# Three moves in the tail of a two-batch layer: tap loads behind the next copy, the next batch's gradient rows loaded mid-tail, the norm's shift a half step ahead

## The chip, the cores and the metric

One core of a Trainium2 chip runs the whole program. The metric is device time in microseconds (us). A run here means one kernel on one chip: one profiled execution and, where I timed it, several more. "Ratio" is the mean time of a kernel's fast executions over the mean of those of the kernel before in the same rounds, so not quite the ratio of the medians that I quote.

## The reference

The reference is the forward pass of one layer and its gradients by `jax.vjp` (x and grad_out of 2 x 4000 x 144, bf16, five taps):

```python
xa = _layernorm(x)                       # (B, T, D) = (2, 4000, 144)
q, k, v = split(xa @ w_qkv)
glob = softmax(q @ k.T * D**-0.5) @ v @ w_att_out
u, g = split(gelu(xa @ w_mlp_in))
loc = (u * depthwise5(_layernorm(g), dw_csgu)) @ w_mlp_out
m = concatenate([glob, loc])
m = m + depthwise5(m, dw_merge)
out = x + m @ w_merge
# returned: out, and the gradients of out against grad_out for x and seven weights
```

## The kernel before

Each batch passes three phases: a head (norm, transposes, taps of the gradient rows), attention (by far the longest, TensorE nearly without a hole: busy 449 of the 460 us from 100 to 560), and a tail, which forms out, the gradient of x and sums for the weights. The tail walks over 16 pairs of 128 rows in half steps `h`; two half steps are a group `g`. These are the parts the change and the argument touch (cuts marked with ...):

```python
def fill(g):                                   # "tap loads"
    for h in range(2):
        r_ = G["r", h, g] = wk.tile([128, 512], BF, tag="r80_%d" % h, name="r80")
        taps[h].load(r_[0:80, :], g * 512, 512, nc.scalar)

def put(g):                                    # the stores they read back
    for h in range(2):
        taps[h].store(G["rs", h][112:128, :], g * 512, 512, nc.scalar)
...
for h in range(NPR + 5):
    g, hf = divmod(h, 2)
    if 0 < h < NPR:
        turn_dx2(*turn_dx(h))                  # 8 transposes, ScalarE copies them to hT
    if hf == 0 and g < NGR:
        turn(g, 0); corr(g, 0); turn(g, 1); corr(g, 1)     # (joined here)
    ...
    if 0 <= h - 1 < NPR:
        sums_act(h - 1); sums_dve(h - 1)
    if hf == 0 and g < NGR:
        put(g)
    if hf == 1 and 0 <= g - 1 < NGR:
        fill(g - 1)
    if nrm:                                    # the norm of the second batch
        for lag, f_ in ((4, nrm.apply), (3, nrm.power), (2, nrm.stats), (1, nrm.load)):
            q, m = divmod(h - lag, 2)
            if m == 0 and 0 <= q < NGR:
                f_(q)
        if NPR <= h < NPR + 3:
            take_go(k, nxt, 1, h - NPR, nrm.ld)  # gradient rows of the second batch
    ...
    if 0 <= h - 1 < NPR:
        means(h - 1)                           # GpSimd: cc, t
    if 0 <= h - 2 < NPR:
        fin(h - 2)                             # VectorE: dxo, then its store on SyncE
    ...
    if hf == 1 and g + 2 < NGR:
        load_dh(g + 2)                         # dhr rows, SyncE
        loads(g + 2)                           # gs and ug rows, SyncE
```

The head's first step for a group transposes the gradient rows `gs` (tile `pm`), has GpSimd extract the last 16 columns of the taps (`g`), transposes these and copies them (`go80f`).

## Time and profile before

| | |
|---|---|
| median, lowest, highest | 1293.03, 1292.06, 1295.48 us (3 executions) |
| profiled span | 1288.0 us |
| first tail, second head, second tail | 85.3, 31.8, 71.5 us |

I cut each trace at four TensorE instructions: the first EF product that waits for GpSimd's g (start of a tail), the head's first pm transpose, attention's first pD product, and the first fH product of the last phase that reads f_ETr. In the lines shown PE is TensorE, DVE VectorE, ACT ScalarE and POOL GpSimd; SPq and ACTq are transfers issued by SyncE and ScalarE; the bracket holds the idle time just before and what ended it.

### The profile page before, as it was taken

To read this page: it belongs to the slowest core of one execution; us is meant where nothing else is said; L and a number is where in the kernel's file an instruction comes from. 1 tells how busy PE (TensorE), PEld (TensorE's weight loads), DVE (VectorE), ACT (ScalarE), POOL (GpSimd) and SP (SyncE) were. 2 spreads that over 40 slices of the span, in tenths; PEclk is the share of its full clock that TensorE was granted. 3 is DMA by queue.
4 is the path that set the end of the run, shared out by engine and by line. 5 is a ranking of instruction groups with operands and counts; after the bars stand their busy time and mean duration, and the time that the engine had idled before them with its cause. 6 is when DMAs were issued, how large, how long until landed. Compare 5 with 4: busy or idle time off the path is not lost.

```text
span 1288.0 us, 39900 instructions
## 1 busy us (share of the span) xinstructions
PE 1211.8 (94%) x15116; PEld 949.9 (74%) x15116; DVE 962.3 (75%) x3293; ACT 843.5 (65%) x2498; POOL 558.8 (43%) x1033
## 2 busy tenths in 40 slices
PE   4899999999999999998989999999999999998996
PEld 2657777777777777788975777777777777778994
DVE  4656778888888788857735677888878878885674
ACT  2667777767767766546646767777777767664542
POOL 6412444545444453257611244444544445324650
PEclk9999999999999999999999999999999999999998
DMA  6378989898989989887775889899888999987861
GB/s 185 88 142 147 156 155 159 155 167 151 161 151 159 170 155 165 151 190 216 202 220 109 152 156 152 153 169 170 148 160 153 154 170 155 164 154 182 238 168 29
DMA packets 634223, 205.51 MB, mean 160 GB/s; under 512 B 577183, under 2 KB 631556, under 8 KB 633988
## 3 DMA queue, kind: packets, MB, share of 16 engines
q1 hardware_dynamic: 627472, 197.54, 80.6%
q10 hardware_dynamic: 6548, 5.33, 1.7%
q8 instruction: 120, 1.97, 0.6%
q14 instruction: 83, 0.68, 0.2%
HBM read 46.22 MB, written 21.79 MB: 53 GB/s over the span
## 4 chain that ended last, share of the span: by engine, by line
PE 71%; DVE 13%; DMA 4%; issue 4%; ACT 4%; POOL 3%; SPq 1%; ACTq 0%; DVEq 0%; POOLq 0%
PE y L1911 15%; PE pS L1865 9%; PE X L1933 9%; PE X L1934 8%; PE pD L1865 7%; PE pS L1861 5%; DVE Sm L1875 5%; PE pc L1573 3%; PE pb L1467 2%; PE po L2088 2%; PE EF L2063 1%; DVE jg L1792 1%; PE gr L2159 1%; DVE acc L1949 1%; ACT Qs L1894 1%
## 5 line engine op out<-in xcount | busy, mean ns | idle before, releaser
L1875 DVE SCALAR_TENSOR_TENSOR Sm<-pD,Pm 128x500 bf16<-128x500 f32 x512 | 325.7, 673 | 80.3 <-PE pD L1865 47.6
L1873 ACT ACTIVATE Pm<-pS 128x500 bf16<-128x500 f32 x512 | 295.5, 586 | 41.2 <-PE pS L1865 38.3
L1933 PE MATMUL X<-Qs,Sm 128*128 128x144 bf16 x2048 | 285.6, 226 | 9.3 <-DVE acc L1949 8.9
L1946 POOL TENSOR_TENSOR acc<-xs,acc 128x432 f32<-128x432 f32 x150 | 168.5, 1123 | 280.5 <-ACT xs L1945 280.0
L1934 PE MATMUL X<-Bt,Pm 128*128 128x144 bf16 x2048 | 285.4, 226 | 0.7 <-DVE Bt L1898 0.7
L1934 PEld LDWEIGHTS <-Pm 128*128 128x128 bf16 x2048 | 199.9, 98 | 11.9 <-issue 11.3
L1933 PEld LDWEIGHTS <-Sm 128*128 128x128 bf16 x2048 | 199.8, 98 | 1.5 <-issue 0.9
L1911 PEld LDWEIGHTS <-PT 128*128 128x128 bf16 x2048 | 136.5, 97 | 30.7 <-issue 2.4
L1911 PEld LDWEIGHTS <-ST 128*128 128x128 bf16 x2048 | 136.4, 97 | 27.6
L1945 ACT COPY xs<-X 128x432 f32<-128x432 f32 x150 | 77.9, 519 | 111.4 <-PE X L1934 103.4
L1949 DVE TENSOR_TENSOR acc<-X,acc 128x432 f32<-128x432 f32 x180 | 104.0, 578 | 53.9 <-PE X L1934 53.2
L1873 ACT ACTIVATION_READ_ACCUMULATOR Pm<-pS 128x1 f32 x512 | 105.0, 205 | 0.0
L1861 PE MATMUL pD<-rb,QBr 16*128 16x500 bf16 x448 | 96.0, 378 | 3.3 <-DVE Sm L1875 2.8
L1865 PEld LDWEIGHTS <-BTm 128*128 128x128 bf16 x512 | 49.8, 98 | 59.9 <-issue 1.6
L1861 PE MATMUL pS<-rb,QBr 16*128 16x500 bf16 x448 | 91.9, 380 | 0.1
L1792 DVE SCALAR_TENSOR_TENSOR jg<-gnC,dgC 128x256 bf16<-128x256 bf16 x160 | 89.6, 560 | 1.0
L1921 POOL TENSOR_TENSOR B_t<-zd,yd 128x144 bf16<-128x144 f32 x64 | 34.0, 531 | 113.0 <-ACT zd L1920 112.7
L1865 PEld LDWEIGHTS <-QTm 128*128 128x128 bf16 x512 | 29.1, 97 | 72.5 <-issue 72.5
L1865 PE MATMUL pS<-rb,QTm 128*128 128x500 bf16 x256 | 76.9, 382 | 0.0
L1865 PE MATMUL pS<-ra,QTm 128*128 128x500 bf16 x256 | 76.5, 381 | 0.0
L1911 PE MATMUL y<-rb,PT 128*128 128x144 bf16 x1024 | 74.3, 226 | 1.0 <-ACT zd L1920 1.0
L1911 PE MATMUL y<-ra,PT 128*128 128x144 bf16 x1024 | 74.3, 226 | 1.1 <-ACT zd L1920 1.1
(626 smaller groups left out, 2895.0 us busy)
## 6 DMA issues: line engine op xcount, KB each, us to landing
gs<-in_grad_out_dram SPq DMA_DIRECT2D x24, 720.0 KB
dh_d<-dh SPq DMA_DIRECT2D x32, 144.0 KB
dhr<-dh_d SPq DMA_DIRECT2D x16, 288.0 KB
gs<-in_grad_out_dram SPq DMA_DIRECT2D x8, 540.0 KB
xg<-in_x_dram SPq DMA_DIRECT2D x21, 144.0 KB
dug_d<-dug SPq DMA_DIRECT2D x16, 144.0 KB
dug<-dug_d SPq DMA_DIRECT2D x32, 72.0 KB
ug_d<-ug SPq DMA_DIRECT2D x32, 72.0 KB
```

Of the source, the lines that this page charges most:

```text
L1573: nc.tensor.matmul(pc[:, q, 0:128], t[:, q * 128 + m:q * 128 + m + 128], W.dg[:, (4 - m) if back else m, :], start=(m == 0), stop=(m == 4))
L1792: nc.vector.scalar_tensor_tensor(jg[:], a_[:, m:m + 256], 1.0, d_[:, 2:258], op0=ALU.mult, op1=ALU.mult, accum_out=dws[:, p, m:m + 1])
L1861: nc.tensor.matmul(o_[h][:, 0:SC], jt[i // 4][2][rr, i % 4, :], S.XR[c2][rr, 0:SC], start=True, stop=False)
L1865: nc.tensor.matmul(o_[h][:, 0:SC], jt[i // 4][w][:, i % 4, :], S.xaT[:, c0:c0 + SC], start=False, stop=True)
L1873: nc.scalar.activation(P[:, pb, c1:c1 + SC], o_[h][:, 0:SC], ACT.Exp, accum_out=ld8[:, 0, n_:n_ + 1])
L1875: nc.vector.scalar_tensor_tensor(Sm[:, pb, c1:c1 + SC], o_[h][:, 0:SC], 1.0, P[:, pb, c1:c1 + SC], op0=ALU.mult, op1=ALU.mult, accum_out=l ...
L1911: nc.tensor.matmul(y[:, w, :], src[:, jj, :], S.xaa[:, j, :], start=(j == 0), stop=(j == NBK - 1))
L1933: nc.tensor.matmul(X[:, jj, :], Sm[:, i % NP, j * 128:(j + 1) * 128], Qs[:, i % 4, :], start=(kk == 0 and jj == 0), stop=False, skip_group ...
L1934: nc.tensor.matmul(X[:, jj, :], P[:, i % NP, j * 128:(j + 1) * 128], Bt[:, i % 4, :], start=False, stop=(kk == 1), skip_group_check=True)
L1945: nc.scalar.copy(xs[:, 0:nj, :], X[:, 0:nj, :])
L1946: nc.gpsimd.tensor_tensor(a_, xs[:, 0:nj, :], a_, op=ALU.add)
L1949: nc.vector.tensor_tensor(a_, X[:, 0:nj, :], a_, op=ALU.add)
```

## The change

Its intent was to take three waits off TensorE's path: the copy of hT no longer stands behind a load on ScalarE, the second batch's rows are there when the head begins, and ScalarE's apply finds its shift ready.

```diff
+    def shift(self, g):
+        nc = self.k.nc
+        mv = self.t[g][1]
+        rs = self.S.rstd_x[:, g * 4:g * 4 + 4]
+        nm = self.sm.tile([128, 4], F32, tag="nmx", name="nm")
+        self.t[g].append(nm)
+        nc.vector.scalar_tensor_tensor(nm[:], mv[:, :, 0], -1.0, rs, op0=ALU.mult, op1=ALU.mult)
+
     def apply(self, g):
         nc = self.k.nc
-        xg, mv = self.t.pop(g)
+        xg, mv, nm = self.t.pop(g)
         rs = self.S.rstd_x[:, g * 4:g * 4 + 4]
-        nm = self.sm.tile([128, 4], F32, tag="nmx", name="nm")
-        nc.vector.scalar_tensor_tensor(nm[:], mv[:, :, 0], -1.0, rs, op0=ALU.mult, op1=ALU.mult)
...
                 nrm.power(g)
+                nrm.shift(g)
                 nrm.apply(g)
...
                     turn_dx2(*turn_dx(h))
+                if hf == 0 and 0 <= g - 2 < NGR:
+                    fill(g - 2)
...
-                if hf == 1 and 0 <= g - 1 < NGR:
-                    fill(g - 1)
...
-                    for lag, f_ in ((4, nrm.apply), (3, nrm.power), (2, nrm.stats), (1, nrm.load)):
+                    for lag, f_ in ((5, nrm.apply), (4, nrm.shift), (3, nrm.power), (2, nrm.stats), (1, nrm.load)):
...
-                    if NPR <= h < NPR + 3:
-                        take_go(k, nxt, 1, h - NPR, nrm.ld)
+                    if h in (9, 11, 13):
+                        take_go(k, nxt, 1, (h - 9) // 2, nrm.ld)
```

Lines of the tail stand 7 further down in the changed kernel: L2063 of before is L2070 of after.

## The prediction

> **What bounds the kernel now.** I began with the page's busy table, which says that TensorE is the bound for the kernel as a whole.
>
> ```profile
> span 1288.0 us, 39900 instructions
> PE 1211.8 (94%) x15116; PEld 949.9 (74%) x15116; DVE 962.3 (75%) x3293; ACT 843.5 (65%) x2498; POOL 558.8 (43%) x1033
> ```
>
> The profiled run has 1288 us, of which some 76 are not TensorE work. Only these can be won, since the change removes no matmul. The change touches the two tails (about 562 to 650 and 1176 to 1288 us) and, through the rows of the second batch, its head (650 to 684). So I took the windows of these stretches. The columns are busy time of TensorE, its weight loads, VectorE, ScalarE and GpSimd, then granted clock, DMA share and GB/s.
>
> ```profile
> 600.00:636.00 36.00, 34.71 (x551) 33.89 (x549) 28.85 (x117) 24.87 (x68) 23.57 (x46) 1.00 0.73 191
> 636.00:650.00 14.00, 14.00 (x227) 14.00 (x225) 6.06 (x23) 4.73 (x15) 6.15 (x11) 1.00 0.90 273
> 650.00:656.00 6.00, 2.21 (x34) 1.99 (x32) 0.57 (x2) 1.63 (x4) 2.09 (x8) 1.00 1.02 305
> 656.00:661.00 5.00, 4.64 (x43) 4.30 (x43) 2.31 (x6) 2.14 (x5) 0.46 (x1) 0.66 0.80 262
> 1206.00:1240.00 34.00, 33.96 (x552) 33.74 (x550) 23.11 (x78) 16.77 (x44) 19.77 (x39) 1.00 0.91 265
> ```
>
> Most of each tail is TensorE without a hole. There is one real hole, 650 to 656, with the DMA engines full, and after it five us at a clock of 0.66. Then I read the chain that ended last around each hole that the change could touch (start, duration, what). First the seam between the batches:
>
> ```profile
> 650.48 5.29 DMA gr_d<-grs
> 655.89 0.43 DVE go80f L1434
> 656.36 0.59 PE pr L1431 x4
> ```
>
> The first copy of the head (go80f) lies in memory that the tail's last store (gr_d, 288 KB) reads, so it waits 5.29 us for that store. The store shares the DMA engines with the gradient rows of the second batch (720 KB a group), issued at 636 to 653. TensorE waits 3.93 us there, plus 0.22 for the rows themselves.
>
> Then the tap loads on ScalarE, in the second tail:
>
> ```profile
> 1197.04 5.57 DMA u<-r
> 1202.64 0.32 ACTq L1527
> 1203.00 1.02 ACT hT L2079
> 1204.06 0.38 PE pt L2039 x4
> ```
>
> The load (L1527) waits for the tap store of the half step before, and the copy of hT stands behind it in ScalarE's order; TensorE then lacks the PSUM buffer. The timeline of TensorE with its idle times gives the same wait as 1.63 us here, 1.04 at 1194.97, and 0.49 at 609.20 in the first tail; elsewhere the copy comes in time.
>
> Last, GpSimd and TensorE in the first tail, from the timelines (the bracket is idle time before, and its releaser):
>
> ```profile
> 612.60 0.30 POOL L2032 TENSOR_SCALAR t3r<-dhr 128x128 bf16<-128x128 bf16 x1 [2.45 <-DMA dhr<-dh_d]
> 613.50 1.14 POOL L2128 TENSOR_SCALAR cc<-ra,n 128x144 f32<-128x144 bf16 x2 [0.60 <-ACT rb L1386]
> 617.01 0.46 POOL L2025 TENSOR_SCALAR g<-gs 128x320 bf16<-128x320 bf16 x1
> 618.02 0.23 PE L2063 MATMUL EF<-Q_t,g 128*80 128x144 bf16 x1
> ```
>
> g is ready at 617.47 and used at 618.02: GpSimd runs only 0.55 us ahead of TensorE in every pair of half steps (598.85 to 599.40 and 607.86 to 608.41 likewise), although it is busy only two thirds of the time. Anything new in its order costs TensorE nearly all of its length.
>
> **What the Trainium skill says.** TensorE: Matmul & The Clock Gate, section "HAM oscillation", asks for no TensorE gaps over about 3.4 us, else the clock halves. The trace agrees: after the 3.93 us gap transposes come every 0.106 us instead of 0.056, to about 659.5; after the 2.41 us gap at 581.95 they don't. The same page, section "Architectural detail", calls ScalarE and VectorE strict FIFO and GpSimd FIFO per core: hT behind the load agrees. DMA: Bandwidth & Descriptors, "Two DMAs through the same engine are not ordered", has the issuing engine wait on the first DMA's semaphore; that is the wait in front of L1527. Its section "Issuing engines are not separate DMA queues" says that all share 16 engines; the 305 GB/s at the seam agrees.
>
> **The change, part by part.** I also compared the order of instructions on each engine.
>
> *Tap loads.* Each pair moves from the middle of an odd half step (some 4 us after the store they wait for) to behind the next even hT copy, about 3 us later. Stores landed after 4.8 to 5.6 us in the chain, so most have landed by then; where one hasn't, the yT copy waits, which TensorE needs only some 2 us later. The loads still come over 4 us ahead of their use. Gain: 1.63 + 1.04 + 0.49 = 3.16 us if nothing else ends the wait. After 1206 TensorE has no slack to lose and the DMA share is 0.91, so I keep 2.5 of the 2.67 in the second tail and 0.4 in the first: **-2.9**.
>
> *Gradient rows, at the seam.* The three loads leave 636 to 653 for 604 to 630, where the windows show 191 GB/s against the 305 reached at the seam. 2.16 MB is about 7 us at 305, and 36 us with 114 GB/s to spare hold 4.1 MB. With the queue empty the gr_d store should take 288 KB at 305 GB/s, 1 us, plus some 1.7 us fixed (a small store in the second tail, f_ETr, took 1.81): land at about 653.2, VectorE's copy to 653.7. The hole shrinks from 3.93 to about 1.5: -2.4, and -0.2 for the rows' own wait. It is then under 3.4 us and the clock stays up; 3.1 us of work at half speed (656.36 to 659.47) become 1.55: -1.5. The fourth group's load still can start only when the first buffer is read, so the head gets tighter for its rows; I give 0.3 back. Together **-3.8**.
>
> *Gradient rows, in the tail.* The scheduled order shows what the diff doesn't. GpSimd's extraction of g for the head's first three groups goes with the loads: it now stands in the tail's GpSimd order, between preparing t3r and the copy of dhr into it, and waits there for each 720 KB load. The first group also puts a memset of 0.70 us ahead of the tail's own g, and the load of dhr now is issued behind the new loads on SyncE. In the first case the memset costs 0.70 - 0.55 = 0.15. SyncE, at 608.19 for dhr before, first must issue four pieces (one behind the memset, at 0.4 us each), so dhr goes out about 2 us later and lands at about 614.7 instead of 612.6; the new g waits to about 612 and is hidden in that. cc then starts at 615.1 instead of 613.5, g follows 1.6 later, less the slack of 0.55: 1.1 us of TensorE. In the second case (from 617.7) 720 KB go ahead of dhr, at 305 GB/s 2.4 us: cc moves by about 1.5, another 1.0. The third extraction comes where GpSimd had 3.27 us idle (before 631.83): nothing. Together **+2.2**.
>
> *Norm shift.* VectorE's order is unchanged to the instruction: nm stays where it was and the apply on ScalarE moves behind it by half a step. It removes seven waits of about 0.5 us (the 7.1 us in ScalarE's table, of which 4.0 is one at the end), and evens the halves (an even half had 1.0 + 2 x 0.6 + 1.0 + 1.7 us of ScalarE work). ScalarE is busy 25 of 36 us there; no hole of TensorE hangs on it: **0**.
>
> Sum: -2.9 - 3.8 + 2.2 = -4.5 us, 1293.0 to **1288.5 us**, -0.35%.
>
> **Rivals.** (1) *GpSimd takes it all back.* If both waits last 4 us instead of 1 to 1.5 (the small pieces of the first group land late behind other traffic; dhr already takes 4.4 us), the first tail loses 6 and the total is 1292 to 1293. For it: the 0.55 us of slack. Against: GpSimd waits for dhr anyway, 2.45 and 1.45 us, and the new waits lie partly beside these. (2) *The seam's wait stays.* go80f waits for a store that the change doesn't move; if its 5.29 us are latency, and not contention, only the loads' own 0.22 goes and the total is 1292. For it: the 144 to 288 KB transfers in the tails take 4 to 5 us, too. Against: those also have 720 KB beside them, and this one lay at 305 GB/s. (3) *Nothing is paid in the tail:* if the extra loads find room, 1286. (4) *The head becomes bound by its loads:* 720 KB in 2.4 us at 305 GB/s against about 3 us of TensorE a group; the margin is thin but there, and would cost 1 us.
>
> **Range and chances.** The sum has two gains that I hold for 80% certain in kind and a loss uncertain by 2 us either way; the runs of before spread over 3.4 us. I take 1285.5 to 1292.0. A gain over 2% would need 26 us, more than all the holes touched here; a loss over 2% would need a deadlock-like stall. So within 2%: 0.98, 0.01 on either side.
>
> **What would show it.** Right: no idle before pt from hT in the second tail (1.63 and 1.04 gone); gr_d landing within 3 us and a hole under 2 us at the seam, clock 1.00 after it; in the first tail two new holes of TensorE, each ended by GpSimd's g, of about 1 us, with GpSimd waiting for the new rows or for dhr; equal length of the attention stages. Wrong: a hole at the seam still over 3.4 us with a slow clock after it, or holes in the first tail that sum to over 4 us, or new idle in the head ended by gradient rows.

## More of the kernel before

The windows between them read, for the kernel before (columns: span; busy time and count of TensorE, its weight loads, VectorE, ScalarE, GpSimd; granted clock, DMA share, GB/s):

```profile
565.94:651.20 85.26, 79.89 (x1263) 77.93 (x1263) 57.83 (x232) 52.02 (x134) 51.99 (x102) 1.00 0.79 219
651.20:683.00 31.80, 27.46 (x294) 22.69 (x292) 13.07 (x39) 18.48 (x49) 5.58 (x16) 0.95 0.60 180
1178.95:1250.46 71.51, 65.93 (x1049) 64.47 (x1050) 47.75 (x160) 36.53 (x96) 41.70 (x85) 1.00 0.76 216
```

Span less TensorE's busy time is TensorE's idle time: 5.37, 4.34 and 5.58 us.

## The result, and the profile after

The changed kernel ran in 1296.65 us (median of 4, 1295.54 to 1297.90), the kernel before in 1294.26 (median of 4, three of them those above). The ratio is 1.002, with a 95% interval of 1.000 to 1.004: the same within 2%, as predicted, but not the 4.5 us faster, and outside the range.

The page and the same windows as in the prediction:

```profile
span 1295.0 us, 39893 instructions
...
PE 1214.0 (94%) x15116; PEld 949.5 (73%) x15116; DVE 961.4 (74%) x3293; ACT 842.9 (65%) x2498; POOL 557.9 (43%) x1033
```

```profile
600.00:636.00 36.00, 32.47 (x508) 31.18 (x506) 25.56 (x102) 22.15 (x58) 24.24 (x47) 1.00 0.91 240
636.00:650.00 14.00, 13.15 (x208) 12.85 (x206) 11.36 (x46) 9.36 (x29) 9.30 (x18) 1.00 0.74 205
650.00:656.00 6.00, 6.00 (x99) 6.00 (x97) 1.64 (x5) 1.70 (x4) 1.73 (x4) 1.00 0.73 197
656.00:661.00 5.00, 5.00 (x82) 4.98 (x80) 0.92 (x2) 0.98 (x3) 0.22 (x1) 1.00 0.26 81
```

The traffic did move out of the seam into 600 to 636 us, where the DMA share rose from 0.73 to 0.91, and TensorE lost 2.2 us of busy time there (34.71 to 32.47; the changed kernel's tail began 4.6 us later, so the windows cover slightly earlier work). By stage:

```profile
570.50:660.24 89.74, 80.63 (x1262) 77.99 (x1263) 57.93 (x232) 50.99 (x134) 52.43 (x105) 1.00 0.80 216
660.24:689.49 29.25, 26.40 (x294) 21.31 (x292) 12.97 (x39) 18.40 (x49) 4.56 (x13) 1.00 0.57 171
1185.91:1257.45 71.54, 66.52 (x1048) 64.47 (x1049) 46.86 (x160) 36.83 (x96) 41.20 (x85) 1.00 0.80 216
```

The first tail is 4.5 us longer, the second head 2.6 shorter, the second tail unchanged. Nearly all of the rest of the 7 us between the two profiles lies ahead of the first tail (565.94 against 570.50), where the two kernels have the same instructions. There the changed kernel's profile has one wait that the other lacks:

```profile
71.31 0.40 PE L1697 MATMUL ph<-w_i,Rz 128*128 128x288 bf16 x1 [3.69 <-DMA Rz<-R_d]
```

I took it for chance and set it aside for a test.

**The seam.** The 3.93 us hole ended by go80f became 1.25 us, and a second one stands after it, which I had not foreseen. TensorE's and GpSimd's timelines after:

```profile
662.33 0.38 PE L1438 MATMUL pr<-w_ident,g 128*80 128x128 bf16 x4 [1.25 <-DVE go80f L1441]
...
666.20 0.79 PE L1474 MATMUL pb<-w_GL,Pm 128*128 128x288 bf16 x5 [1.29 <-POOL Pm L1413]
```

```profile
665.25 0.46 POOL L1435 TENSOR_SCALAR g<-gs 128x320 bf16<-128x320 bf16 x1 [6.15 <-DMA gs<-in_grad_out_dram]
```

GpSimd sat 6.15 us in front of the fourth group's extraction, waiting for its rows. The head's memsets of Pm's edges came behind it in GpSimd's order, so TensorE's product on Pm waited for a memset of 0.10 us. The chain that ended last there goes back to those rows' load (4.44 us): rival (4) of the prediction, a head bound by its loads, came true in part.

**The second tail.** The waits for hT (1.04 and 1.63 us) are gone, as predicted. In their place:

```profile
1235.62 0.22 PE L2070 MATMUL EF<-ug,gs 128*128 128x144 bf16 x1 [0.92 <-DMA ug<-ug_d]
...
1246.06 0.22 PE L2070 MATMUL EF<-ug,gs 128*128 128x144 bf16 x1 [1.12 <-DMA ug<-ug_d]
```

**The first tail.** The two holes that I had expected to be ended by GpSimd's g are ended by the tail's own rows (gs 1.41 us at 625.15, ug 0.77 at 635.57). SyncE's timelines show why these came late. Before:

```profile
607.29 0.84 SPq L1089 DMA_DIRECT2D out_dram<-dxo  x1
608.19 0.50 SPq L2021 DMA_DIRECT2D dhr<-dh_d  x1
608.79 0.40 SPq L1112 DMA_DIRECT2D gs<-in_grad_out_dram  x1
609.28 0.46 SPq L2017 DMA_DIRECT2D ug<-ug_d  x1
```

After, with the new rows' four pieces just ahead (612.66 to 614.9):

```profile
614.92 0.41 SPq L1089 DMA_DIRECT2D out_dram<-dxo  x1
615.93 0.36 SPq L2028 DMA_DIRECT2D dhr<-dh_d  x1
617.78 0.38 SPq L1112 DMA_DIRECT2D gs<-in_grad_out_dram  x1
618.26 0.45 SPq L2024 DMA_DIRECT2D ug<-ug_d  x1
```

Counted from the start of each tail, ug is issued at 43.3 us before and at 47.8 after, 4.4 us later.

### The profile page after: what moved, and what is told of

The parts are those of the page before. It is cut to its first block, busy times and chain, and to the rows that moved or that the text cites. A ratio compares the mean times of both kernels' runs of the same rounds, so it can differ in the third digit from the quotient of the medians.

```text
span 1295.0 us, 39893 instructions
## 1 busy us (share of the span) xinstructions
PE 1214.0 (94%) x15116; PEld 949.5 (73%) x15116; DVE 961.4 (74%) x3293; ACT 842.9 (65%) x2498; POOL 557.9 (43%) x1033
## 4 chain that ended last, share of the span: by engine, by line
PE 69%; DVE 13%; DMA 7%; issue 4%; ACT 4%; POOL 2%; SPq 1%; ACTq 0%; DVEq 0%; POOLq 0%
PE y L1918 15%; PE pS L1872 9%; PE X L1940 8%; PE X L1941 8%; PE pD L1872 7%; PE pS L1868 5%; DVE Sm L1882 5%; DMA ug<-ug_d 3%; PE pc L1580 2%; PE pb L1474 2%; PE po L2095 1%; PE EF L2070 1%; DVE jg L1799 1%; PE gr L2166 1%; DVE acc L1956 1%
## 5 line engine op out<-in xcount | busy, mean ns | idle before, releaser
L1872 PE MATMUL pD<-rb,BTm 128*128 128x500 bf16 x256 | 75.3, 376 | 0.0
```

Of the source, the lines that this page charges most:

```text
L1872: nc.tensor.matmul(o_[h][:, 0:SC], jt[i // 4][w][:, i % 4, :], S.xaT[:, c0:c0 + SC], start=False, stop=True)
```

## The experiments

All stages of all traces, in us. "Idle" is span less TensorE's busy time. A star marks a first tail with a stretch of 3.41 us at a granted clock of 0.50 that begins 0.4 to 1.3 us after the end of the hole of 2.41 to 2.51 us near its start. Its busy time is then 81.6 us on average instead of 80.2, so its length isn't comparable, and its idle time only roughly: a wait of 0.73 to 0.86 us for GpSimd's g, 24 to 25 us into the tail, stands in eight of the nine tails without a star (0.15 in no_shift) and in none of the eleven with one. Idle time also has a part that is chance: waits for the first rows, 7 to 9 us into the first tail and ahead of all that F, R, S and O change there, add up to anything from 0 (before, fill_only, mid_own, late_own) to 1.52 us (late_own_again). Parts: F tap loads moved, R rows earlier (9: half steps 9, 11, 13; 13: half steps 13, 14, 15), S shift, O head's extractions in the head's own buffer, H dhr rows half a step earlier.

| run | parts | ratio to before, 95% | 1st tail, idle | 2nd head, idle | 2nd tail, idle |
|---|---|---|---|---|---|
| before | | | 85.26, 5.37 | 31.80, 4.34 | 71.51, 5.58 |
| after | F R9 S | 1.0020 [1.000, 1.004] | 89.74, 9.11 | 29.25, 2.85 | 71.54, 5.02 |
| fill_only | F | 0.9985 [0.9969, 1.0002] | 86.36, 6.50 | 32.82, 4.82 | 73.16, 6.30 |
| rows_only | R9 | 1.0000 [0.9980, 1.0021] | 88.75, 8.31 | 29.39, 2.98 | 72.45, 6.35 |
| shift_only | S | 1.0051 [1.0035, 1.0067] | 90.90, 10.75 | 32.63, 5.23 | 72.68, 6.57 |
| rows_late | R13 | 0.9993 [0.9974, 1.0012] | 88.27*, 6.83 | 29.42, 2.92 | 69.84, 3.86 |
| no_shift | F R9 | 1.0019 [0.9997, 1.0042] | 88.39, 8.07 | 29.52, 3.13 | 70.09, 4.04 |
| no_rows | F S | 1.0017 [0.9990, 1.0043] | 86.58*, 5.21 | 32.40, 5.13 | 70.50, 4.16 |
| after_again | F R9 S | 0.9996 [0.9978, 1.0014] | 89.61*, 7.60 | 29.32, 2.92 | 71.91, 5.90 |
| fill_rows_late | F R13 | 0.9994 [0.9972, 1.0016] | 89.81*, 8.17 | 29.52, 3.12 | 71.41, 5.16 |
| mid_own | R9 O | 0.9986 [0.9970, 1.0002] | 87.89*, 6.21 | 28.13, 1.67 | 72.28, 6.17 |
| late_own | R13 O | 0.9963 [0.9945, 0.9980] | 87.41*, 5.97 | 27.94, 1.48 | 72.52, 6.60 |
| light | (wrong) | 0.9988 [0.9968, 1.0007] | 86.07, 6.03 | 33.22, 4.99 | 71.29, 5.14 |
| light_fill | F (wrong) | 0.9994 [0.9972, 1.0015] | 88.41*, 6.65 | 30.70, 3.24 | 72.16, 6.00 |
| dh_early | H | 1.0010 [0.9987, 1.0033] | 85.82, 5.83 | 33.23, 4.87 | 73.53, 7.59 |
| dh_fill | F H | 1.0019 [0.9998, 1.0039] | 88.79*, 7.31 | 33.52, 5.53 | 70.03, 3.70 |
| best | R13 O H | 0.9987 [0.9965, 1.0008] | 88.37*, 6.71 | 28.17, 1.55 | 72.77, 6.76 |
| best_fill | F R13 O H | 0.9998 [0.9974, 1.0022] | 90.05*, 8.28 | 28.04, 1.45 | 68.56, 2.48 |
| combo | F R13 S O H | 0.9982 [0.9967, 0.9998] | 87.84, 7.17 | 27.87, 1.44 | 70.13, 3.72 |
| late_own_again | R13 O | 0.9989 [0.9969, 1.0010] | 89.34*, 7.61 | 27.96, 1.51 | 71.40, 5.48 |

Each timed ratio of the experiments rests on six executions (dh_fill five) against eleven of before; that of after rests on four against four. The intervals are 0.3 to 0.5% wide, 4 to 7 us, while the effects sought are 1 to 5 us; so the stages of the traces carry most of the argument, and each trace is one execution.

### First set: one part at a time

My theory at this point (A and B in the expectations): the second tail is held by when its rows arrive, and the rows loaded mid-tail delay the tail's own rows. The rival was my prediction's: GpSimd's extractions take the time.

**fill_only**: the `fill` lines of the diff alone.

> The kernel before with the tap loads alone moved behind the next copy. My prediction's step: -2.9 us, of which 2.5 in the second tail (holes of TensorE ended by ScalarE's hT at 1.04 and 1.63 us vanish) and 0.4 in the first, so about 1290 to 1291 us. Theory A, from the profile of the whole change: the second tail is held by when its own rows arrive, so the wait for hT is only exchanged for waits on ug and gs rows; second tail (first EF product to first fH product) stays at 72.7 us within 0.5, first tail changes by under 0.7, ratio 1.000 within 0.001.

It measured 1294.7 against 1296.31 us. The second tail stayed long (73.16), with waits for gs and ug in place of hT, as theory A expected; the first tail did not gain 0.4 but had 6.50 us idle against 5.37. TensorE's two waits in the second tail of before, then what stands in fill_only:

```profile
1194.97 0.38 PE L2039 MATMUL pt<-w_ident,ug 128*128 128x128 bf16 x4 [1.04 <-ACT hT L2079]
...
1204.06 0.38 PE L2039 MATMUL pt<-w_ident,ug 128*128 128x128 bf16 x4 [1.63 <-ACT hT L2079]
```

```profile
1206.00 0.24 PE L2063 MATMUL EF<-Q_t,gs 128*128 128x144 bf16 x1 [0.45 <-DMA gs<-in_grad_out_dram]
...
1206.59 0.22 PE L2063 MATMUL EF<-ug,gs 128*128 128x144 bf16 x1 [0.35 <-DMA ug<-ug_d]
...
1235.99 0.22 PE L2063 MATMUL EF<-ug,gs 128*128 128x144 bf16 x1 [1.06 <-DMA ug<-ug_d]
```

**rows_only**: the `take_go` lines alone.

> The kernel before with the second batch's gradient rows alone loaded at half steps 9, 11 and 13 in place of 16, 17 and 18. My prediction's step: first tail +2.2 through GpSimd's added extractions, start of the second head -3.8, so -1.6 us. Theory B, from the profile of the whole change: the three loads delay the tail's own rows; first tail +4 to +5 us with new holes of TensorE ended by DMA of gs and ug between 60 and 80 us after its start, second head -2.7, so +1.5 to +2.3 us, ratio 1.001 to 1.002. If instead the first tail's loss came with the moved tap loads, this run shows the first tail within 1 us of the kernel before and the time 2 to 3 us shorter.

Ratio 1.0000. The first tail lost 2.9 us of idle time (8.31 against 5.37), the head gained 2.4 us of its length. The loss stays with the rows and does not need the moved tap loads; 0.85 us of it is the chance wait for the first rows. Theory B's sign, holes ended by gs and ug 60 to 80 us into the tail, did not show: the largest new hole (1.72 us, 55.7 us into the tail) is ended by hT.

**shift_only**: `shift` at lag 4, `apply` at lag 5, nothing else.

> The kernel before with the norm shift alone made a half step ahead. My prediction's step: 0. Expected by both theories: ratio 1.000 within 0.001, first tail within 0.5 us, no new hole. If the later apply of the norm (lag 5, not 4) is what moved the first tail in the changed kernel, the first tail is over 2 us longer here.

This was the surprise: 1302.05 against 1296.31 us, the only kernel that is clearly slower. The part I had given 0 costs some 6 us alone as timed, and some 5 us of idle time in the first tail. Its first tail:

```profile
567.97:658.87 90.90, 80.15 (x1262) 77.97 (x1263) 57.74 (x232) 52.09 (x134) 51.89 (x102) 1.00 0.75 203
```

ScalarE's timeline and, in the second fence, TensorE's tell how:

```profile
592.42 1.70 ACT L1392 ACTIVATE rb<-xg,nm,rstdx 128x144 bf16<-128x144 bf16 x4 [1.69 <-POOL rstdx L1376]
594.02 0.99 ACT L2086 COPY hT<-pt 128x1024 bf16<-128x1024 bf16 x1
```

```profile
595.07 0.38 PE L2046 MATMUL pt<-w_ident,ug 128*128 128x128 bf16 x4 [1.88 <-ACT hT L2086]
```

The apply (rb) takes 1.70 us. It moved from the even half steps into the odd ones, just ahead of the even step's hT copy, where the two tap loads already stand. Even half steps have three groups of transposes for two PSUM buffers, so the third one (ug) waits for hT. Five such waits (1.88, 0.66, 0.67, 1.72, 0.60) make 5.5 us of the 5.6 us by which this first tail is longer.

**rows_late**: `if h in (13, 14, 15)`, after the tail's own last gradient rows are issued at 11.

> The kernel before with the second batch's gradient rows loaded at half steps 13, 14 and 15: after the tail's own last gradient rows (issued at 11) but three half steps ahead of before. Theory B (contention with the tail's own rows): the first tail stays within 1 us of before, the second head still gains 2 to 3 us, so 2 to 3 us faster than before, ratio 0.998. Rival (GpSimd's extraction ahead of its own work in the tail takes the time): the first tail loses 2 us or more in holes ended by GpSimd, and nothing is gained.

The head gained as much as with the rows at 9 (29.42); the first tail's idle time is 6.83. The length of 88.27 is outside what theory B expected, but holds a stretch of half clock. In time it is not distinguishable from before.

### Second set: the change less one part, and the change again

**no_shift**: the changed kernel without S.

> The changed kernel without the norm shift: tap loads behind the next copy and gradient rows at half steps 9, 11, 13, the norm as before. Theory C, formed from the shift alone (which was 0.5% slower): the later apply puts ScalarE's 1.70 us of activations into the odd half steps, just ahead of the next step's hT copy, and costs time with the other two parts too; then this is 2 to 5 us faster than the whole change. Theory B (the rows' contention with the tail's own loads makes the loss): the same as the whole change within 1 us, its first tail 88 to 90 us.

**no_rows**: the changed kernel without R.

> The changed kernel without the earlier gradient rows: tap loads behind the next copy and the norm shift. Theory C, the shift costs in itself: first tail over 88 us, 3 us or more slower than the moved tap loads alone. Rival to C: the shift is harmless once the tap loads have left the odd half steps, since these then hold the apply in place of the loads; then the first tail is 85 to 87 us and the time that of the moved tap loads alone within 1 us, and the shift was made for the moved loads.

no_shift is not faster than the whole change, so theory C (the shift costs in any company) fell. In no_rows the first tail is idle 5.21 us, as little as anywhere, against 6.50 with F alone and 10.75 with S alone (of the difference from F alone some 0.85 may be the star's). The waits for hT that S alone brought, 5.5 us, are down to 0.85. The rival to C held in the trace, although the timed ratio (1.0017) is too wide to confirm it: once the tap loads have left the odd half steps the apply fits there, and the two moves belong together.

**after_again**: the changed kernel, word for word.

> The changed kernel once more, word for word, beside the two above on one chip: ratio 1.002 within 0.002 as before. Its profile tells what of the start of the first tail (570.5 us against 565.9, where the instructions are the same) is chance: by the theory that it is, this one starts anywhere from 565 to 573; by the rival that the change shifts it, at 570 or later. First tail 89 to 91 us, second head 29 to 30.

Ratio 0.9996, after 1.002 at first. The change is worth nothing that these runs can see, in either direction. Its first tail starts at 567.41 us, not 570.50, without the wait for Rz. Over all 20 traces, with the same instructions up to there, the start lies anywhere from 565.94 to 572.88, and nine of them have a wait of 2.6 to 3.8 us for Rz. That part of the difference between the two profiles was chance.

**fill_rows_late**: F with the rows at 13, 14, 15.

> A candidate: tap loads behind the next copy, gradient rows at half steps 13, 14, 15, no norm shift. If the gains of the moved tap loads (ratio 0.9985) and of the later rows (0.9993, second head 2.4 us shorter) add up: ratio 0.997 to 0.998, first tail 86 to 88 us, second head 29.4, second tail 71 to 73. Rival (the tail is full: what leaves one queue waits in another): ratio 0.999 to 1.000.

Ratio 0.9994; the gains did not add up, as the rival said: 8.17 us idle in the first tail.

### Third set: transfers or GpSimd, and a lighter second tail

**mid_own** and **late_own**: rows at 9, 11, 13 or at 13, 14, 15, and one edit in the head:

```diff
-            g80 = ld.tile([128, 4, 80], BF, tag="g80")
+            g80 = (wk if b else ld).tile([128, 4, 80], BF, tag="g80")
```

The buffer now belongs to a pool that opens after the tail. The instruction order confirms that the three extractions leave the tail's GpSimd order and that Pm's memsets are ahead of them again.

> The kernel before with the gradient rows at half steps 9, 11, 13, but the head's extractions g of the second batch in a buffer of the head's own pool, so that GpSimd makes them after the tail (checked in the instruction order) and only the transfers sit in the tail. Theory B (transfers contend with the tail's own rows): first tail as in the run of the rows alone, 88 to 89 us. Rival (GpSimd's three extractions inside the tail cost it): first tail 85 to 86.5 us. By both: the seam's hole ended by go80f 1.2 to 2.5 us, no hole ended by GpSimd's memset of Pm, head 28 to 31 us.

```profile
571.25:659.14 87.89, 81.68 (x1262) 79.61 (x1263) 57.43 (x232) 51.92 (x134) 51.56 (x102) 0.98 0.80 220
```

The same loads at the same half steps leave 6.21 us idle in place of the 7.60 to 9.11 in the four traces with the extractions inside the tail (mean 8.27), against 5.74 on average without earlier rows (before, light, dh_early). Taken as they stand, some 2 of about 2.5 us would go with GpSimd's extractions and 0.5 with the transfers, and the rival would have the better of theory B. But this is one trace with a star, and it doesn't bear that out. The one starred trace with these rows inside the tail and the extractions too is after_again; without the chance wait for the first rows it has 6.43 us, against 6.21 here. And what the extractions should have delayed is as late without them: ug is issued 48.2 us after the tail's start in mid_own (47.1 to 49.2 with the extractions, 43.3 in before), and GpSimd turns to the dhr rows of that group at 49.5 (48.8 to 50.8; 46.7 in before). So the earlier rows make these steps late without the extractions too; how TensorE's loss divides between the two isn't shown. In the head the hole at Pm's memset is gone (28.13), and also the one ended by go80f, which I had expected to stay; in their place TensorE waits 0.82 us for ScalarE's copy of Pm.

> The same with the rows at half steps 13, 14, 15, a candidate: neither the transfers before the tail's own last rows nor the extractions in the tail. First tail 85.3 to 86.5 us if no clock dip falls in it (1.7 us each), head 28 to 30, so 2 to 3 us faster, ratio 0.998. Rival: what the seam gains, the tail loses again to the transfers, ratio 1.000.

Ratio 0.9963, 1292.72 against 1297.20 us: the first version that is faster beyond its interval.

**light** and **light_fill**: in the second tail the reload of the first batch's sums is replaced by zeros from GpSimd; six of the nine outputs are wrong by it (relative error near 0.7; I had expected one).

> The kernel before without the reload of the first batch's sums (1.2 MB by the sizes of the two arrays) in the second tail, zeros in their place, so one output is wrong on purpose. It is one half of a pair. By itself: the second tail 70 to 72 us, its holes ended by hT still there.

> The other half of the pair: the same lighter second tail with the tap loads behind the next copy (one output wrong on purpose). Theory A (in the second tail the moved loads gain nothing because its own rows arrive no sooner): with the queue lighter, fewer holes ended by gs and ug, and the second tail 1.5 to 2.5 us shorter than in the pair's other half. Rival (what gives way to what is not a matter of how full the queues are): the second tail within 0.7 us of the other half and the same holes ended by gs and ug, over 2 us in sum.

The pair is inconclusive. The second tails are 71.29 and 72.16, and the edit brought its own wait: GpSimd's memsets held up VectorE's t, which cost TensorE 0.84 us in one and 2.20 in the other. It was a badly built control, since it put work on an engine that stands in the path.

### Fourth set: what stands in front of the rows

GpSimd waits 16.3 us in the second tail of before for the dhr rows, which are issued together with gs and ug, just ahead of them. The edit issues them half a step earlier:

```diff
+                if hf == 0 and g + 2 < NGR:
+                    load_dh(g + 2)
                 if hf == 0 and g < NGR:
                     put(g)
...
-                    load_dh(g + 2)
                     loads(g + 2)
```

> The kernel before with each load of dhr rows (the rows GpSimd waits for, 2.45 us once in the first tail) issued half a step earlier, ahead of the stores that hold the queue. Theory D (loop: dhr late, GpSimd late, the gradient outputs late, the next gs and ug rows late): GpSimd's waits on dhr fall below 1 us, gs and ug issued earlier, few holes ended by them; by itself ratio 0.998 to 1.000, since the hT waits remain in the second tail, 70 to 72 us. Rival: no change in anything but GpSimd's own waits, ratio 1.000.

> The same plus the tap loads behind the next copy. Theory D: now the moved tap loads pay, second tail 1.5 to 2.5 us shorter than with early dhr rows alone (68.5 to 70 us), few holes ended by gs or ug. Rival (the rows are late for another reason: their own buffers or the transfers' length): second tail within 0.7 us of the other, 1 to 3 us of holes ended by gs and ug still in it.

> Candidate: gradient rows of the second batch at half steps 13, 14, 15, the head's extractions in the head's own buffer (this pair alone had ratio 0.9963), and dhr rows half a step earlier. Theory D: ratio 0.994 to 0.996. Rival, early dhr rows give nothing: 0.996 to 0.997. First tail 85 to 87 us, head 28 us.

> The same with the tap loads behind the next copy. If they pay once the dhr rows are early: ratio 0.002 below the candidate without them. If not: equal within 0.0015, and the moved loads are worth nothing in either tail.

GpSimd's waits for dhr rows in the second tail fell from 16.3 to 2.8 us in dh_early, as theory D said, but the second tail got no shorter by it (73.53, where 70 to 72 was expected): the waits for hT stayed. best, at 0.9987, missed its 0.994 to 0.996.

Second tails of dh_early, then of dh_fill, then of best_fill:

```profile
1188.62:1262.15 73.53, 65.94 (x1048) 64.45 (x1049) 45.78 (x160) 36.54 (x96) 42.55 (x85) 1.00 0.76 210
```

```profile
1186.70:1256.73 70.03, 66.33 (x1048) 64.43 (x1049) 47.62 (x160) 36.84 (x96) 41.80 (x85) 1.00 0.80 221
```

```profile
1184.05:1252.61 68.56, 66.08 (x1049) 64.45 (x1050) 48.12 (x160) 36.69 (x96) 41.71 (x85) 1.00 0.81 225
```

With early dhr rows the moved tap loads do pay: 73.53 to 70.03, and 72.77 to 68.56 in the other pair. Without them they don't: seven traces with F have a mean of 5.23 us idle, eight without F 5.72. What they share is where the wait goes. After the first group, waits for gs and ug add up to 2.35 us in the second tail of fill_only and 2.19 in after; to 0.30 in dh_fill and to none in best_fill. (In all seven traces with F and late dhr rows they are 0.57 to 2.54.) So the rows were the wall behind hT. How the early dhr rows clear it I can't fully say. Theory D said that gs and ug would be issued earlier, and they are: counted from the tail's start, ug of four groups in turn at 15.4, 23.4, 31.9 and 41.4 us in dh_fill, at 16.7, 25.2, 34.4 and 44.6 in fill_only. But TensorE comes earlier too. From that issue to its first EF product on ug it is 6.4, 6.6, 6.9 and 7.8 us in fill_only, with a wait for ug at three of the four, and 5.8, 6.9, 8.4 and 7.9 in dh_fill, with none. So in the first of these groups the rows landed sooner after their issue, in the third they were issued well ahead of their use. That 288 KB less go just ahead of them is a likely part of it, argued and not shown.

The timed ratios did not follow (1.0010 to 1.0019, 0.9987 to 0.9998). In the traces the first tail gives back 1.5 and 1.6 us of idle time of the 3.9 and 4.3 that the second wins, and what is left is less than the half width of the timed intervals (2.7 to 3.1 us). ScalarE in the first tail of best_fill:

```profile
592.76 0.44 ACTq L1527 DMA_DIRECT2D r<-u  x1
...
595.53 0.32 ACTq L1520 DMA_DIRECT2D y<-r  x1
599.08 0.40 ACTq L1520 DMA_DIRECT2D u<-r  x1
599.52 1.70 ACT L1386 ACTIVATE rb<-xg,nm,rstdx 128x144 bf16<-128x144 bf16 x4 [4.15 <-DMA y<-r]
601.13 0.99 ACT L2079 COPY hT<-pt 128x1024 bf16<-128x1024 bf16 x1
```

The second tap store is issued 3.55 us after the first, and the apply and the next hT stand behind it; TensorE then waits 1.78 us for hT at 602.17. By the semaphores of the trace this store waited for the u load of 592.76, which landed at 598.98. The loads now go out some 3 us ahead of the next stores, in place of some 4, and these wait for them: summed over the first tail, ScalarE's tap stores wait 3.2 to 8.7 us for tap loads in the ten traces with F, and 0 to 0.65 in nine of the ten without (2.22 in mid_own). So the wait has only moved, from loads behind stores to stores behind loads. With the shift (no_rows) the apply is not in that half step.

### Last set: everything together

**combo**: F, S, R13, O and H. **late_own_again**: late_own once more.

> Tap loads behind the next copy, norm shift, gradient rows at half steps 13, 14, 15, the head's extractions in its own buffer, dhr rows half a step earlier. If the parts add as read from the traces: first tail 85 to 86.5 us (1.7 more with a clock dip), second head 28, second tail 68.5 to 70; so 5 to 8 us faster than before, ratio 0.994 to 0.996. Rival, the first tail takes the second's gain back as in the candidate without the shift: first tail 88 us or more without a clock dip, ratio 0.998 to 1.000.

> The candidate of the rows at 13, 14, 15 with the head's own buffer, once more: ratio 0.9963 within 0.002 if that result holds. If the chips and executions spread more than the intervals say: 0.998 to 0.999.

combo: 1292.16 against 1294.19 us, ratio 0.9982, interval just below 1; less than expected. Its head (27.87) and second tail (70.13) came as expected, its first tail did not: 7.17 us idle, of which 0.85 is ended by GpSimd's g (as in before) and 0.93 by hT (0.49 in before). late_own_again: 0.9989, so the 0.9963 was partly luck. Both versions stand about 0.2% ahead of before, and these runs can't tell which is the better; against the changed kernel they were compared only through before.

## Why the prediction was wrong

**What held.** The verdict (within 2%). The bound of each stage. The seam's mechanism: hole under 2 us, clock at 1.00 after it. The clock step is confirmed by all traces: after a seam hole of 3.06 to 4.64 us the clock fell in 8 of 8, after holes of up to 1.5 us in 0 of 12. The 305 GB/s at the seam, which the prediction calls agreement with shared DMA engines, is only consistent with it; no run here shows the sharing itself.

**Near in size, not by the path foreseen.** The rows' cost in the tail was predicted as +2.2 by way of GpSimd; rows_only has 8.31 us idle against a mean of 5.74, so +2.6 (+1.9 without the chance waits for the first rows). But the two holes ended by GpSimd's g near the start of the tail are the same in before and in rows_only (2.41 and 0.85 us) and no new one came (one of 1.34 us did in rows_late); the new holes are ended by hT and gs there, by gs, ug and hT in the changed kernel. And in mid_own the tail's own rows are as late without GpSimd's extractions. That the size came out near is partly luck.

**The clock, more closely.** The clock records in the traces explain the stars. Up to the last 9 us of the program, every stretch at clock 0.50 lasts 3.413 or 6.827 us (54 stretches), and all stretches of one trace start whole multiples of 3.413 us apart, on a grid that lies differently in each trace. In the eleven starred tails one interval of this grid takes so much of the hole that TensorE works only 0.90 to 1.31 us in it, and the next interval is slow; in the other nine the hole is split between two intervals, TensorE works at least 1.54 us in each, and the clock stays up. One interval and the next in no_rows, then in combo:

```profile
581.65:585.06 3.41, 1.00 (x17) 0.81 (x15) 2.63 (x9) 2.20 (x6) 3.07 (x7) 1.00 0.35 82
585.06:588.47 3.41, 3.41 (x33) 3.41 (x31) 2.13 (x11) 1.31 (x5) 2.01 (x5) 0.50 0.90 272
```

```profile
584.64:588.06 3.42, 1.63 (x27) 1.63 (x28) 1.73 (x6) 1.98 (x5) 3.17 (x6) 1.00 0.56 121
588.06:591.47 3.41, 3.41 (x59) 3.41 (x57) 3.17 (x18) 1.50 (x4) 1.58 (x5) 1.00 1.02 331
```

So which tails lose 1.4 us to the clock is chance of the grid. It is not the whole rule: some 710 us in (seven traces) and between 1040 and 1080 us (three) the clock fell after intervals with 1.7 to 3.1 us of TensorE work.

**The step that failed** is the tap loads, "I keep 2.5 of the 2.67 in the second tail and 0.4 in the first". The mean idle time of the second tail fell by 0.5 us (5.72 to 5.23), within the spread of either group, not by 2.5. I had argued that TensorE "has no slack to lose" there and a DMA share of 0.91, and took the first for a promise that the gain stays. It was the second that counted: the rows arrived just in time for a TensorE that waits for hT, and late for one that doesn't. In the first tail the moved loads alone cost about 1.1 us (6.50, 6.65 and 7.31 idle against 5.74), where the next stores now wait for them (3.2 to 8.7 us of ScalarE's time, above). The prediction had asked whether the loads come in time for their use, and not what stands behind them.

**Mis-sized terms.** The seam, -3.8: eight heads without earlier rows have a mean of 32.54 us, six with R and without O 29.40, so -3.1. The missing 0.7 is less than the new wait of 1.3 us for Pm's memset behind GpSimd's extraction, which I had not looked for in the head's order and which goes back to the head's own loads. The norm shift, 0: right for the whole change (8.07 us idle without it, 9.11 and 7.60 with it), for a reason that I didn't have. Alone it costs 5 us; it is free only because the tap loads left its half step.

**The sum.** With its mean of 8.36 us idle in two traces the changed kernel's first tail loses 2.6, the head gains 3.1, the second tail gains 0.3 (5.46 against 5.72): -0.8 us in place of -4.5. Timed, it was 2.6 us slower by the means of the first runs and 0.5 faster in the second, so zero within what these runs resolve.

**The range.** I took 1293.0 as the base; beside the experiments the same kernel had medians of 1294.2 to 1297.2. A range 6.5 us wide around a base known to 3 us was too narrow even for a right mechanism.

**Still open.** How early dhr rows shorten the waits for gs and ug; the split of the rows' cost between GpSimd and transfers, which one trace of mid_own doesn't settle; and what else than TensorE's working time in an interval moves the clock.

## What to carry to other kernels

Before you count a removed wait as gained, ask what ends next behind it: list, for the same instruction, when each of its other inputs arrives, and take the gain only up to the second latest. A move between half steps is also a move of load between them; count each in-order engine's work per half step before and after, for the loads, the stores and the compute together, and ask what will wait for the moved transfer in its turn. And look in the scheduled order for what an earlier load drags along on other engines: here the pool of a single buffer put three extractions into the tail, and memsets of the head behind a wait for rows.

## What the Trainium skill lacked or had wrong

- TensorE: Matmul & The Clock Gate. The rule of thumb in "HAM oscillation" (no gaps over about 3.4 us) is not a safe limit here. After a hole of 2.41 to 2.51 us near the start of the first tail the clock fell to 0.50 for 3.41 us in 11 of 20 traces and not in the other 9, at a cost of 1.4 us of TensorE time (81.6 against 80.2). The same page's "Part 1: The HAM clock gate" says that the activity window is 3413 ns long and runs freely; the traces agree (54 stretches of 3.413 or 6.827 us on one grid a trace). What it lacks is how little work in a window lets the clock fall: here 1.31 us of TensorE work and less did, 1.54 and more did not, in this stage. My prediction read one trace as agreement with the rule.
- No page that I read gives the spread of one kernel's executions on one core. Here the same kernel had 1290.5 to 1299.6 us over all chips, and the first tail started up to 6.9 us apart with the same instructions ahead of it, so that a change of 0.3% needs more than six executions.
